# Attention mix on one core: free choice of engine for PSUM copies, planned PSUM banks, a reordered start and a split last tile

## Chip, cores, metric

The kernel runs on one core of a Trainium2 chip (trn2). The metric is device time in microseconds, the median of several executions. Short names: PE is the tensor engine (TensorE), PEld its weight loads, ACT is ScalarE, DVE is VectorE, POOL is GpSimd, SP is the queue that issues most DMAs. A "group" is the eight 128x512 matmuls that fill one PSUM bank.

All runs quoted here are in the fast state. Still, executions of one kernel differ by up to 0.9% here, and a part of the argument is about that. I use two measures side by side: the timed runs, and stretches between fixed landmarks of PE's instruction stream in the profiled run.

## The reference

```python
x = A_x; g = sigmoid((x * gate_w).sum(-1, keepdims=True))      # x: 1 x 2048 x 1024, bf16
a = linear_attention(x, A_wqkv, A_wo)    # 32 heads of 32; phi(t) = where(t > 0, t + 1, exp(t)) + 1e-6
#   kv = phi(k)^T v,  z = sum phi(k),  o = phi(q) kv / (phi(q) z + 1e-6),  a = o @ wo
b = local_attention(x, B_wqkv, B_wo)     # window of 8 keys at distance 2, softmax
return g * a + (1 - g) * b
```

## The kernel before

A small scheduler sorts operations: each has an engine, an assumed cost and what it reads and writes; the scheduler plays the program with these costs and emits each engine's order with semaphores. Program order gives priority. The parts that matter, with cuts:

```python
load_x(0, 0)                                   # x tiles come transposed, by SP
for d in range(0, 8, 2): load_w(0, 0, Bw, 2048, 1, d, d + 2, "act")   # first half of the v weights, 4 x 256 KB
for d in range(0, 8, 4): load_w(0, 1, Bw, 2560, 2, d, d + 4, "act")   # second half, 2 x 512 KB
for t in range(1, NT): load_x(t, 3 + t)
main = Ring(banks[0:7])                        # banks in rotation
for t in range(NT):                            # v of the local attention, both halves of a tile in turn
    for half in range(2): ...                  # a group, then copy to ACT (half 0) or DVE (half 1)
# ... gate matmuls ...
SO = banks[4:8]; OB = banks[3]                 # scores; fixed bank for P @ V
main = Ring(banks[0:3])                        # three rotating banks for the rest
def fill(e_, b, gr):                           # one block of the local attention
    # S: 16 row-tiled matmuls -> ACT exp -> DVE mask
    def values():
        db, _ = main.next()                    # P @ V into OB and the sums into db: one PE operation
        # ACT Ln, ACT Exp, DVE multiply into qT
    later.append((slot_n[0] + 2, values))      # two slots later
# k copies on ACT, q copies on DVE; after each tile of the linear attention: after(2, state)
# ... linear stage ...
for n, (u, j) in enumerate(nums):              # 32 numerator groups
    numer(u, j)      # group, phi (ACT exp, two DVE ops), DVE running maximum, later a "den" matmul, ACT Ln and Exp, DVE multiply
    if n == 3: turn()                          # transposes of kv, one DVE copy of 1024 columns
    if 6 <= n < 14: fold(n - 6, 0); fold(n - 6, 1)
    if n >= 17: a_out(*outs.pop(0))            # first output groups
# after(8 if u == 0 else 2, over): distance from a numerator to its den
# ... last stage: 16 tiles, each two groups, a DVE operation, a store
```

## Time and profile before

| | before |
|---|---|
| time, median of 3 runs at first | 519.6 us (519.31 to 521.1) |
| span of the profiled run | 518.7 us |
| PE busy | 504.4 us, 97% |
| first gate matmul (end of the v stage) | 67.01 us |
| kv transposes | 346.06 us |
| first output group | 375.79 us |

The page of the kernel before, first the engines' busy time, then the chain that ended last:

```profile
PE 504.4 (97%) x4385; PEld 229.8 (44%) x4385; DVE 276.3 (53%) x477; ACT 232.0 (45%) x342; POOL 4.7 (1%) x21
...
PE 92%; DVE 5%; DMA 2%; ACT 1%; ACTq 0%; issue 0%
```

PE is the bound. 256 groups at 1.73 us are 442 us of its time, and other matmuls are most of the remaining 62 us. No part of the change takes a matmul away, so everything must come from the 14.3 us of the span in which PE is idle (the start, waits, the tail) and from time lost inside its busy share (half clock, changes of mode, waits that the profile does not list). All of PE's waits, in total, number of times, and the longest:

```profile
PE ps_all L1253 <- DMA w_4_52<-in_B_wqkv_dram: 3.0, 2, 2.1
PE ps_all L1253 <- ACT ra_54_102 L1523: 1.8, 3, 1.1
PE ps_all L1284 <- DVE warm_72 L1203: 1.3, 1, 1.3
PE ps_all L1253 <- DMA xT_49<-in_A_x_dram: 0.9, 1, 0.9
PE ps_all L1253 <- DVE pk_46_94 L1262: 0.7, 1, 0.7
PE ps_all L1253 <- DVE pk_47_95 L1262: 0.7, 1, 0.7
PE ps_all L1521 <- DVE p_51_99 L1262: 0.5, 1, 0.5
PE ps_all L1253 <- ACT L_37_85 L1381: 0.3, 1, 0.3
PE ps_all L1253 <- DVE kva_68 L1451: 0.2, 1, 0.2
```

w_4 and xT are the start; pk, L and kva belong to the attention stage (a group waits until a bank has been read out); ra and p belong to the linear stage. The start itself, PE's timeline in the first 14 us (start, duration, what, and the idle time ahead of it):

```profile
6.02 1.04 PE L1253 MATMUL ps_all<-w_4_52,xT_49 128*128 128x512 bf16 x4 [0.88 <-DMA xT_49<-in_A_x_dram]
7.99 0.78 PE L1253 MATMUL ps_all<-w_4_52,xT_49 128*128 128x512 bf16 x2 [0.93 <-DMA w_4_52<-in_B_wqkv_dram]
10.87 3.59 PE L1253 MATMUL ps_all<-w_4_52,xT_49 128*128 128x512 bf16 x8 [2.10 <-DMA w_4_52<-in_B_wqkv_dram]
```

Eight matmuls from 10.87 us on take 3.59 us, twice their usual time: the clock had dropped. The window table shows it in the column before the DMA share (granted clock, 1.00 is full):

```profile
6.00:11.70 5.70, 2.65 (x9) 0.66 (x10) 0.00 (x0) 0.00 (x0) 0.00 (x0) 0.70 1.17 201
11.70:14.80 3.10, 3.10 (x9) 1.09 (x8) 0.00 (x0) 0.60 (x1) 0.00 (x0) 0.50 1.21 305
```

Not all waits are listed as such, since the ends of matmuls are modelled. In the timeline a tiled block of 16 is followed 0.22 us later by a block of its own mode (tiled in the same way) and 0.31 to 0.32 us later by one of another mode. Here the last one is followed only 0.55 us later (257.99 to 258.54 us), which I read as a hidden wait of 0.23 us; the profile names no cause for it.

```profile
257.57 0.38 PE L1443 MATMUL ps_all<-az_48_96,pk_46_94 128*32 128x33 bf16 x32
257.78 0.40 PE L1372 MATMUL ps_all<-E_33_81,v_38_86 128*32 128x114 bf16 x16
257.99 0.40 PE L1376 MATMUL ps_all<-E_33_81,ones_58 128*32 128x114 bf16 x16
258.54 0.82 PE L1253 MATMUL ps_all<-w_4_52,xT_49 128*128 128x512 bf16 x3
```

In the linear stage the other engines are full. The window from the kv transposes to the first output group (columns: window, its length, PE, PEld, DVE, ACT, POOL busy, clock, DMA): DVE is busy 29.43 of 29.73 us.

```profile
346.06:375.79 29.73, 27.34 (x128) 11.56 (x127) 29.43 (x66) 27.34 (x50) 0.00 (x0) 1.00 0.00 1
```

### The profile page before, as it was taken

Reading aid. Unit: us, or ns where it says so; the run is one execution under the profiler, and the core shown is the slowest. Engines: PE = TensorE matmul, PEld = TensorE weight load, DVE = VectorE, ACT = ScalarE, POOL = GpSimd, SP = SyncE. Lnnn points to the kernel's source line nnn. Section 1 sums busy time; section 2 is a strip of 40 time slices with the busy share of each in tenths; the row PEclk is TensorE's granted clock in tenths of the full one; section 3 lists DMA queues with packets and bytes.
Section 4 is the critical chain, followed back from the end, with each engine's and each line's share of the span. In section 5 each row is a group of like instructions: output and inputs, shape, how many; then the busy total and the mean of one; then the engine's idle time right before and its main releaser. Section 6 shows DMA issues by size and latency. Waiting matters only on the chain.

```text
span 518.7 us, 9927 instructions
## 1 busy us (share of the span) xinstructions
PE 504.4 (97%) x4385; PEld 229.8 (44%) x4385; DVE 276.3 (53%) x477; ACT 232.0 (45%) x342; POOL 4.7 (1%) x21
## 2 busy tenths in 40 slices
PE   6999999999999999999999999998999999999996
PEld 1444444444444444444444444443344444444442
DVE  0122235567676778466454544369986664334443
ACT  1111111355555567677675755348975653210000
POOL 3000000000000000000000000000000000000000
PEclk8999999999999999999999999999999999999999
DMA  9998790003300023001010100310000000002212
GB/s 201 209 236 297 232 323 3 2 22 101 104 21 21 23 92 123 23 13 32 13 32 11 33 11 3 126 38 1 0 2 0 2 0 1 1 23 81 82 65 81
DMA packets 47227, 34.81 MB, mean 67 GB/s; under 512 B 21957, under 2 KB 43205, under 8 KB 47178
## 3 DMA queue, kind: packets, MB, share of 16 engines
q1 hardware_dynamic: 45034, 32.01, 21.5%
q10 hardware_dynamic: 2144, 2.10, 1.6%
q8 instruction: 36, 0.59, 0.5%
q14 instruction: 13, 0.11, 0.1%
HBM read 21.51 MB, written 8.40 MB: 58 GB/s over the span
## 4 chain that ended last, share of the span: by engine, by line
PE 92%; DVE 5%; DMA 2%; ACT 1%; ACTq 0%; issue 0%
PE ps_all L1253 84%; PE ps_all L1354 2%; PE ps_all L1372 2%; DMA w_4_52<-in_B_wqkv_dram 2%; PE ps_all L1376 1%; PE ps_all L1443 1%; PE ps_all L1521 1%; DVE mx_57_105 L1211 1%; DVE w_5_53 L1281 1%; DVE pq_8_56 L1525 1%; DVE pq_8_56 L1262 1%; PE ps_all L1313 0%; ACT e_27_75 L1259 0%; DVE xT_49 L1525 0%; DVE kva_68 L1451 0%; DVE e_27_75 L1260 0%
## 5 line engine op out<-in xcount | busy, mean ns | idle before, releaser
L1253 PE MATMUL ps_all<-w_4_52,xT_49 128*128 128x512 bf16 x512 | 118.2, 385 | 5.9 <-DMA w_4_52<-in_B_wqkv_dram 3.0
L1253 PE MATMUL ps_all<-xT_49,w_6_54 128*128 128x512 bf16 x512 | 119.2, 380 | 1.8 <-ACT ra_54_102 L1523 1.8
L1253 PEld LDWEIGHTS ps_all<-w_4_52,xT_49 128*128 128x128 bf16 x512 | 48.9, 98 | 67.4 <-DMA w_4_52<-in_B_wqkv_dram 4.2
L1253 PEld LDWEIGHTS ps_all<-xT_49,w_6_54 128*128 128x128 bf16 x512 | 48.2, 98 | 60.6 <-ACT ra_54_102 L1523 3.5
L1253 PE MATMUL ps_all<-w_7_55,xT_49 128*128 128x512 bf16 x256 | 60.5, 380 | 0.3 <-ACT L_37_85 L1381 0.3
L1253 PE MATMUL ps_all<-xT_49,w_5_53 128*128 128x512 bf16 x256 | 58.6, 379 | 0.0
L1253 PE MATMUL ps_all<-w_7_55,qT_50 128*128 128x512 bf16 x256 | 55.4, 379 | 0.0
L1279 ACT ACTIVATE kT_51<-ps_all 128x512 bf16<-128x512 f32 x32 | 19.1, 597 | 60.5 <-PE ps_all L1253 60.5
L1253 PE MATMUL ps_all<-w_5_53,xT_49 128*128 128x512 bf16 x192 | 42.7, 379 | 0.0
L1253 PEld LDWEIGHTS ps_all<-w_7_55,qT_50 128*128 128x128 bf16 x256 | 25.0, 98 | 30.2
L1253 PEld LDWEIGHTS ps_all<-xT_49,w_5_53 128*128 128x128 bf16 x256 | 24.4, 98 | 29.4 <-issue 0.4
L1253 PEld LDWEIGHTS ps_all<-w_7_55,xT_49 128*128 128x128 bf16 x256 | 23.5, 98 | 27.7 <-ACT L_37_85 L1381 0.5
L1417 DVE TENSOR_SCALAR qT_50<-ps_all 128x512 bf16<-128x512 f32 x32 | 22.0, 688 | 13.6 <-PE ps_all L1253 13.4
L1253 PEld LDWEIGHTS ps_all<-w_5_53,xT_49 128*128 128x128 bf16 x192 | 18.8, 98 | 22.7
L1359 ACT ACTIVATE E_33_81<-ps_all 128x1824 bf16<-128x1824 f32 x12 | 20.2, 1687 | 4.7 <-PE ps_all L1354 4.6
L1211 DVE TENSOR_TENSOR mx_44_92<-mx_44_92,kT_51 128x1024 bf16<-128x1024 bf16 x16 | 11.0, 690 | 21.1 <-ACT kT_51 L1279 21.1
L1359 ACT ACTIVATE E_34_82<-ps_all 128x1824 bf16<-128x1824 f32 x12 | 20.2, 1686 | 2.1 <-PE ps_all L1354 2.1
L1359 ACT ACTIVATE E_35_83<-ps_all 128x1824 bf16<-128x1824 f32 (+1 forms) x12 | 20.1, 1677 | 2.1 <-PE ps_all L1354 2.1
L1259 ACT ACTIVATE e_25_73<-ps_all 128x512 bf16<-128x512 f32 x22 | 13.1, 596 | 17.4 <-PE ps_all L1253 17.4
L1451 DVE TENSOR_TENSOR kva_68<-ps_all,kva_68 128x264 f32<-128x264 f32 x15 | 6.5, 433 | 26.3 <-PE ps_all L1443 26.3
L1362 DVE TENSOR_TENSOR E_35_83<-E_35_83,msk_59 128x1824 bf16<-128x1824 bf16 (+1 forms) x12 | 13.2, 1100 | 12.4 <-ACT E_35_83 L1359 12.4
L1259 ACT ACTIVATE e_26_74<-ps_all 128x512 bf16<-128x512 f32 x21 | 12.5, 597 | 15.9 <-PE ps_all L1253 15.9
(156 smaller groups left out, 521.6 us busy)
## 6 DMA issues: line engine op xcount, KB each, us to landing
w_5_53<-in_B_wqkv_dram SPq DMA_DIRECT2D x2, 1024.0 KB, 7.5
w_6_54<-in_B_wqkv_dram SPq DMA_DIRECT2D x2, 1024.0 KB, 7.7
w_7_55<-in_A_wqkv_dram SPq DMA_DIRECT2D x2, 1024.0 KB, 6.0
w_4_52<-in_A_wqkv_dram SPq DMA_DIRECT2D x2, 1024.0 KB, 10.1
w_5_53<-in_A_wo_dram SPq DMA_DIRECT2D x2, 1024.0 KB, 5.7
w_6_54<-in_A_wqkv_dram SPq DMA_DIRECT2D x2, 1024.0 KB, 5.9
w_7_55<-in_B_wo_dram SPq DMA_DIRECT2D x2, 1024.0 KB, 6.5
out_dram<-o_55_103 SPq DMA_DIRECT2D x8, 256.0 KB, 2.0
```

The lines of the kernel that those rows point to most:

```text
L1211: P.op("dve", lambda e, m=m, op=op: e.tensor_tensor(m[:, 0:n], m[:, 0:n], src, op), 0.08 + n / 1920.0, reads=[m.all(), reg], writes=[m.all()],
L1253: last = e.matmul(bank.ap(), lhs(dc), rhs(dc), start=(dc == 0), stop=(dc == 7))
L1259: P.op("act", lambda e: e.activation(e_[:, :], bank.ap(), ACT.Exp), act(512), reads=[bank.iv], writes=[e_.all()])
L1262: P.op("dve", lambda e: e.scalar_tensor_tensor(out=dst, in0=bank.ap(), scalar=0.0, in1=e_[:, :], op0=ALU.max, op1=ALU.add), dps(512), read ...
L1279: P.op("act", lambda e: e.activation(dst, bank.ap(), ACT.Copy), act(512), reads=[bank.iv], writes=[reg])
L1281: P.op("dve", lambda e: e.tensor_copy(dst, bank.ap()), dps(512), reads=[bank.iv], writes=[reg])
L1354: last = e.matmul(SO[j].ap(c * nq, (c + 1) * nq), kT[32 * j:32 * j + 32, c0 + c, t0 + k0:t0 + k0 + 128], qT[32 * j:32 * j + 32, c0 + c, t0 ...
L1359: P.op("act", lambda e: e.activation(E[:, :, 0:nq].rearrange("p (j c) q -> p j c q", j=4), ps[:, 4:8, 0:4 * nq].rearrange("p j (c q) -> p ...
L1362: P.op("dve", lambda e: e.tensor_tensor(E[:, :, 0:nq], E[:, :, 0:nq], msk[:, mi:mi + 1, 0:nq].to_broadcast([128, 16, nq]), ALU.mult), 0.15 ...
L1372: e.matmul(OB.ap(c * nq, (c + 1) * nq)[32 * j:32 * j + 32, :], vt[:, (4 * c + j) * 32:(4 * c + j) * 32 + 32], E[:, 4 * j + c, 0:nq], start ...
L1417: P.op("dve", lambda e, dst=dst, bank=bank: e.tensor_scalar(dst, bank.ap(), SCALE, None, op0=ALU.mult), dps(512), reads=[bank.iv], writes= ...
L1451: P.op("dve", lambda e: e.tensor_tensor(kva[:, :, :], src(), kva[:, :, :], ALU.add), dps(264), reads=[bank.iv, kva.all()], writes=[kva.all()])
```

## The change

The intent: let no PSUM copy wait for a busy engine and no group for a bank. A copy goes to ACT or DVE, whichever the scheduler finds free first; banks come from a pool by an earlier pass of the plan (up to six passes); PV and sums are two operations; the scheduler charges for mode changes of PE; v starts with first halves only; the last tile is split. Cut to its core, indentation aside:

```diff
+        def ready(o, at):
+            if o.eng == "any":          # engine chosen when the operation becomes ready
+                ...
+                o.eng = min(est)[1]
...
+                if o.mode != mode:
+                    t += 0.09
...
-    for d in range(0, 8, 2):
-        load_w(0, 0, Bw, 2048, 1, d, d + 2, "act")
-    for d in range(0, 8, 4):
-        load_w(0, 1, Bw, 2560, 2, d, d + 4, "act")
+        load_w(0, 0, Bw, 2048, 0.1, 0, 2, "act")
+        load_w(0, 0, Bw, 2048, 0.2, 2, 4, "act")
+        load_w(0, 0, Bw, 2048, 0.3, 4, 6)
+        load_w(0, 0, Bw, 2048, 0.4, 6, 8)
...
+        for t, half in [(4 * b + i, half) for b in range(NT // 4) for half in range(2) for i in range(4)]:
...
+            if (t, half) == (0, 0):
+                load_w(0, 1, Bw, 2560, 1, 0, 4, "act", [o])      # only after the first group
+                load_w(0, 1, Bw, 2560, 2, 4, 8, "act", [o])
...
-    OB = banks[3]
-    main = Ring(banks[0:3])
+        main = Pool(banks[0:4])
...
-        later.append((slot_n[0] + 2, values))
+            after(3, values, True)
...
-                after(2, lambda t=t, pkt=pkt, azt=azt: state(t, pkt, azt))
+                    states.append((slot_n[0] + 4, lambda t=t, pkt=pkt, azt=azt: state(t, pkt, azt)))
...
+            for i in range(2):           # kv transposes leave PSUM in two copies
+                move(kvT[:, 4 * i:4 * i + 4, :].rearrange("p i c -> p (i c)"), ...
...
-        top((2,), p_, preg, 512)         # running maximum on DVE
+            phi(bank, p_, preg, 8 * u + j)   # accumulated by ACT's exponential instead
...
-        after(8 if u == 0 else 2, over)
+            after(6 if u == 0 else 2, over)
...
-        if n == 3:
+            if n == 1:
             turn()
-        if 6 <= n < 14:
+            if 3 <= n < 11:
...
+            parts = [(0, 512), (512, 1024)] if t < NT - 1 else [(0, 512), (512, 768), (768, 1024)]
```

The one-line description of the change did not mention the changed distances (three slots, four slots, `n == 1`, folds from 3) nor the maxima. The rate at which blocks of the local attention are handed out (`FILL`) went from 0.34 to one third per slot. A slot is one step of the program, one group of k, q or the linear stage.

## The prediction

> **What bounds it now.** TensorE. The page shows PE busy 504.4 of 518.7 us; the chain that ended last is 92% PE. By the table of forms and the timeline, the dense work is 256 groups of eight 128x512 matmuls at 1.73 us, 442 us. The change removes none of them. What can shrink:
>
> 1. Start. The waits give 3.9 us for the first weights and x tile. Continuous work begins at 10.87 us, and by the window table the granted clock is 0.50 from 11.7 to 14.8 us: nine matmuls at 427 ns, 1.9 us lost. The Trainium skill ("TensorE: Matmul & The Clock Gate", the HAM clock gate) has an idle window drop the clock to half[...].
> 2. Attention stage, 195 to 330 us: recorded PE waits of 1.9 us (ACT L, pk, kva) and three more inside "busy" (a 16-matmul block followed after 0.55 instead of 0.32 us). PE waits for one of three rotating banks, or PV's fixed bank.
> 3. Linear stage, 346 to 370 us: 8 groups and 30 single matmuls need 20.3 us (estimate from 1.73 and 0.216 us) and take 23.7. The chain here is a string of DVE operations.
> 4. Tail: the last matmul ends at 514.3 us; 0.75 us of DVE, a DMA and the closing follow.
>
> **What the change does.**
> - Start: the first four half tiles need 1 MB of weights, not 2, and the second half is issued only after the first group. Two pieces go behind x0 on the other queue. The first group should finish near 8 instead of 11.7 us. But four x tiles are now wanted 1.73 us apart while the second half competes; at the 202 GB/s of the first 13 us, 3 MB are not in before 14 us. I expect new short waits on xT and w. Net gain 3.0 us (1 to 5).
> - Attention: sums and PV become two operations on banks of one pool of four; values come a slot later, state two. I expect 2.0 us of the 2.6.
> - Linear: 32 running maxima leave DVE (0.43 us each here, 14 us), replaced by accumulation in ACT's exponentials; four R tiles, not two; folds go to either engine. ACT plus DVE then just fit beside PE. Gain 2.0 us.
> - Tail: last DVE step on 256 columns, 0.3 us.
> - Mode switches: the instruction order has 147 instead of 144 changes among plain, row-tiled and column-tiled matmuls, though the scheduler now charges for them. Each costs about 0.1 us (a 16-matmul block lasts 0.22 us before its own mode, 0.32 before another). The skill ("TensorEngine Tiling", Key Properties) says changing mode drains the engine; the trace agrees. Cost 0.3 us.
> - Choosing ACT or DVE for k, q and v copies gains nothing: PE does not wait between 16 and 195 us.
>
> **Sum.** 519.6 - 3.0 - 2.0 - 2.0 - 0.3 + 0.3 = 512.6 us, 1.3% faster; range 509.0 to 515.8. Faster by over 2%: 0.15; within 2%: 0.84; slower: 0.01.
>
> **What would show it.** Right: PE busy nearly unchanged; group one ends near 8 us, short PE waits on xT or w before 18 us, gate matmuls 3 us before 67.1; waits for pk, kva, L under 1 us in all; kv transposes to first output group 2 us shorter. Wrong: PE waits beyond 20 us; attention gaps stay; ACT leads the chain after 330 us (accumulating exponentials well over 0.75 us).
>
> **What would make it wrong.** The start is the largest and least certain term: if second-half weights starve the x tiles, it gains nothing; if the clock stays full and transfers overlap well, 5 us. The planned order rests on fixed costs; if they are off, new waits appear elsewhere.

## The result

The changed kernel took 512.84 us (512.26 to 514.8, 4 runs) against 519.77 us (519.31 to 521.1, 4 runs). The ratio is 0.9869, 95% interval 0.9836 to 0.9903. Ratios here are the mean time of one kernel's runs over that of the other's of the same rounds, so not quite the ratio of the medians. The prediction of 512.6 us holds.

The page of the changed kernel, the same parts:

```profile
PE 502.4 (98%) x4393; PEld 231.4 (45%) x4393; DVE 277.6 (54%) x462; ACT 224.3 (44%) x359; POOL 4.7 (1%) x21
...
PE 95%; DMA 2%; SPq 1%; DVE 1%; ACT 0%; issue 0%
```

All of PE's waits:

```profile
PE ps_all L1315 <- DMA xT_49<-in_A_x_dram: 4.3, 3, 3.4
PE ps_all L1354 <- DVE warm_72 L1265: 1.3, 1, 1.3
PE ps_all L1570 <- ACT kvT_94 L1347: 0.7, 1, 0.7
```

The waits of the attention stage are gone, and one is left in the linear stage. In the start, waits for weights have been traded for waits for x tiles:

```profile
5.93 2.00 PE L1315 MATMUL ps_all<-w_4_52,xT_49 128*128 128x512 bf16 x8 [0.66 <-DMA xT_49<-in_A_x_dram]
8.17 5.35 PE L1315 MATMUL ps_all<-w_4_52,xT_49 128*128 128x512 bf16 x24 [0.24 <-DMA xT_49<-in_A_x_dram]
16.91 5.44 PE L1315 MATMUL ps_all<-w_4_52,xT_49 128*128 128x512 bf16 x18 [3.38 <-DMA xT_49<-in_A_x_dram]
```

The first group ends at 7.9 us, as predicted, and four groups run at full clock. Then PE waits 3.38 us for the fifth x tile, which took 8.43 us to land (in the chain: start, duration, what), and the clock drops to half again after 16 us (same columns as above):

```profile
8.35 8.43 DMA xT_49<-in_A_x_dram
```

```profile
15.00:16.00 1.00, 0.00 (x0) 0.00 (x0) 0.00 (x0) 0.00 (x0) 0.00 (x0) 1.00 1.75 216
16.00:16.90 0.90, 0.00 (x0) 0.02 (x1) 0.00 (x0) 0.00 (x0) 0.00 (x0) 0.70 0.80 162
16.90:18.00 1.10, 1.09 (x3) 0.41 (x4) 0.00 (x0) 0.00 (x0) 0.00 (x0) 0.50 1.17 260
```

The linear stage, from kv transposes to first output group:

```profile
339.74:370.38 30.64, 29.98 (x146) 13.56 (x145) 26.91 (x53) 27.59 (x62) 0.00 (x0) 1.00 0.00 1
```

The two kernels run different numbers of numerator groups before these landmarks (7 and 5 before the transposes, 11 and 13 between transposes and first output group). So I subtract 1.727 us for each and call what is left A (gate matmuls to transposes) and L (transposes to first output group):

| stretch of the profiled run, us | before | changed | difference |
|---|---|---|---|
| start to first gate matmul | 67.01 | 66.75 | -0.26 |
| A | 266.96 | 264.36 | -2.60 |
| L | 10.73 | 8.19 | -2.54 |
| first output group to the end | 142.91 | 142.42 | -0.49 |
| span | 518.7 | 512.8 | -5.9 |

The profiled run of the changed kernel is the slowest of its four (514.8 us); the others have spans of 510.3 to 511.3 us at a clock of 0.999 or 1.000, the profiled one 0.995.

L has a floor: 0.44 us of transposes, then 16 folds and 15 denominators at 0.216 us, 7.13 us (with the 16 denominators of the changed kernel 7.35). So the kernel before lost 3.6 us there, the changed one 0.8, most of it the 0.66 us for kvT.

### The profile page after: what moved, and what is told of

Its sections match the earlier page's. It is cut to its first block, busy times and chain, and to the rows that moved or that the text cites. A ratio compares the mean times of both kernels' runs of the same rounds, so it can differ in the third digit from the quotient of the medians.

```text
span 512.8 us, 9938 instructions
## 1 busy us (share of the span) xinstructions
PE 502.4 (98%) x4393; PEld 231.4 (45%) x4393; DVE 277.6 (54%) x462; ACT 224.3 (44%) x359; POOL 4.7 (1%) x21
## 4 chain that ended last, share of the span: by engine, by line
PE 95%; DMA 2%; SPq 1%; DVE 1%; ACT 0%; issue 0%
PE ps_all L1315 75%; PE ps_all L1667 11%; PE ps_all L1444 4%; PE ps_all L1426 2%; DMA xT_49<-in_A_x_dram 2%; PE ps_all L1592 1%; SPq L1287 1%; PE ps_all L1513 1%; PE ps_all L1570 1%; DVE pq_8_56 L1328 0%; PE ps_all L1386 0%; DVE zbd_67 L1552 0%; SPq L1292 0%; DVE kvbd_66 L1553 0%; ACT e_25_73 L1324 0%
## 5 line engine op out<-in xcount | busy, mean ns | idle before, releaser
L1315 PE MATMUL ps_all<-w_4_52,xT_49 128*128 128x512 bf16 x512 | 117.1, 383 | 4.3 <-DMA xT_49<-in_A_x_dram 4.3
L1315 PE MATMUL ps_all<-xT_49,w_6_54 128*128 128x512 bf16 x512 | 118.3, 379 | 0.0
L1315 PEld LDWEIGHTS ps_all<-w_4_52,xT_49 128*128 128x128 bf16 x512 | 48.7, 98 | 64.3 <-issue 5.9
L1315 PE MATMUL ps_all<-w_7_55,xT_49 128*128 128x512 bf16 x256 | 59.7, 380 | 0.1
L1315 PE MATMUL ps_all<-xT_49,w_5_53 128*128 128x512 bf16 x256 | 58.6, 379 | 0.0
L1667 PE MATMUL ps_all<-w_7_55,qT_50 128*128 128x512 bf16 (+1 forms) x264 | 55.4, 373 | 0.0
L1315 PE MATMUL ps_all<-w_5_53,xT_49 128*128 128x512 bf16 x192 | 42.7, 379 | 0.0
L1347 ACT ACTIVATE kT_51<-ps_all 128x512 bf16<-128x512 f32 x19 | 11.3, 597 | 32.1 <-PE ps_all L1315 32.1
L1350 ACT ACTIVATE qT_50<-ps_all 128x512 bf16<-128x512 f32 x19 | 11.3, 597 | 29.9 <-PE ps_all L1315 29.9
L1349 DVE TENSOR_SCALAR xT_49<-ps_all,g_63 128x512 bf16<-128x512 f32 x15 | 11.2, 750 | 19.9 <-PE ps_all L1315 19.9
L1346 DVE CAST kT_51<-ps_all 128x512 bf16<-128x512 f32 x13 | 9.0, 689 | 17.4 <-PE ps_all L1315 17.4
L1434 DVE TENSOR_TENSOR E_38_86<-E_38_86,msk_59 128x1824 bf16<-128x1824 bf16 x12 | 13.2, 1103 | 5.7 <-ACT E_38_86 L1431 5.7
L1350 ACT ACTIVATE xT_49<-ps_all,g_63 128x512 bf16<-128x512 f32 x9 | 6.2, 687 | 22.9 <-PE ps_all L1315 22.9
```

The costliest lines, as they stand in the source:

```text
L1315: last = e.matmul(bank.ap(), lhs(dc), rhs(dc), start=(dc == 0), stop=(dc == 7))
L1346: fd = lambda e: e.tensor_copy(dst, src())
L1347: fa = lambda e: e.activation(dst, src(), ACT.Copy)
L1349: fd = lambda e: e.tensor_scalar(dst, src(), scale, None, op0=ALU.mult)
L1350: fa = lambda e: e.activation(dst, src(), ACT.Copy, scale=scale)
L1434: P.op("dve", lambda e: e.tensor_tensor(E[:, :, 0:nq], E[:, :, 0:nq], msk[:, mi:mi + 1, 0:nq].to_broadcast([128, 16, nq]), ALU.mult), 0.15 ...
```

## The experiments

Twelve kernels ran, all with correct results. Their edits are shown cut to the lines that matter. They ran in four sets, on three chips, each beside the kernel before, so compare ratios rather than medians. "Gate to end" is the span less the time of the first gate matmul; it leaves the start out. The kernel before has 451.7 us, the changed kernel 446.05.

| run | time, median (range), us | ratio to before | gate | A | L | gate to end |
|---|---|---|---|---|---|---|
| changed | 512.84 (512.26 to 514.80) | 0.9869 | 66.75 | 264.36 | 8.19 | 446.05 |
| e1_old_start | 514.76 (514.68 to 515.25) | 0.9903 | 67.07 | 264.36 | 8.19 | 446.1 |
| e2_paced | 512.09 (511.43 to 514.27) | 0.9869 | 63.06 | 265.18 | 7.34 | 446.3 |
| e3_keep_warm | 512.81 (511.95 to 513.18) | 0.9869 | 64.14 | 264.37 | 8.18 | 445.9 |
| e4_fixed | 514.14 (512.80 to 515.36) | 0.9893 | 64.85 | 263.73 | 8.43 | 445.9 |
| e5_pv_bank | 513.85 (2 runs) | 0.9874 | 66.64 | 264.11 | 7.19 | 445.4 |
| e6_old_slots | 518.53 (2 runs) | 0.9963 | 66.93 | 266.76 | 8.58 | 449.2 |
| e7_mx_back | 516.84 (2 runs) | 0.9931 | 66.87 | 264.35 | 9.31 | 447.2 |
| e9_linear_old | 513.88 (2 runs) | 0.9874 | 65.98 | 264.72 | 7.14 | 445.8 |
| b1_positions | 517.30 (516.92 to 517.33) | 0.9944 | 66.22 | 265.26 | 10.00 | 449.1 |
| b2_halves | 518.01 (517.03 to 519.99) | 0.9959 | 68.62 | 265.27 | 10.15 | 449.3 |
| e10_pace8 | 512.65 (512.18 to 513.03) | 0.9858 | 64.05 | 264.37 | 8.19 | 446.4 |
| e11_best | 510.84 (510.06 to 514.69) | 0.9837 | 63.26 | 264.11 | 7.13 | 445.0 |

One caution holds for all of them: every edit makes the scheduler plan the whole order anew. e2 touches only the start, yet its A is 0.82 us longer and its L 0.85 us shorter than in the changed kernel. So a difference in A or L of that size need not come from the line that was edited.

### e1_old_start: the changed kernel with the old start

```diff
-        load_w(0, 0, Bw, 2048, 0.3, 4, 6)       # and the other three of this kind
+        for d in range(0, 8, 2): load_w(0, 0, Bw, 2048, 1, d, d + 2, "act")
+        for d in range(0, 8, 4): load_w(0, 1, Bw, 2560, 2, d, d + 4, "act")
-            if (t, half) == (0, 0):             # and its two loads
-        for t, half in [(4 * b + i, half) for b in range(NT // 4) for half in range(2) for i in range(4)]:
+        for t, half in [(t, half) for t in range(NT) for half in range(2)]:
```

> The changed kernel with the old start: loads, prompt second half of the weights, and both halves of one tile after another. Theory: the start is worth 0.3 us where the clock dropped after the 3.4 us wait for the fifth x tile (as in the profiled run of the changed kernel: gate matmuls at 66.75 against 67.08 us) and about 2.4 us where it did not. So here the gate matmuls start at 66.9 to 67.3 us, granted clock about 0.992, time 514.0 to 514.6 us (changed kernel 512.3 to 512.9), and the times of its runs scatter less than the changed kernel's. Rival: the new start is worth its 3 us always, and the profiled run only misread it: then 515.5 or more.

Measured: gate at 67.07 us, A and L exactly as in the changed kernel, 514.76 us, and all four runs within 0.6 us. So the new start is worth about 1.8 us in the timed runs (0.9903 less 0.9869, times 519.7 us), between the two figures expected; the intervals of the two ratios overlap (0.9888 to 0.9919 here), so this is rough. That the new start brings the scatter is not shown: the kernel before has the old start, and its nine runs of the same rounds spread over 1.9 us (519.28 to 521.16). The rival (3 us always) falls. The granted clocks were 0.993 to 0.999, so my figure of 0.992 was no constant.

### e2_paced: second half of the weights in quarters

```diff
-            if (t, half) == (0, 0):
-                load_w(0, 1, Bw, 2560, 1, 0, 4, "act", [o])
-                load_w(0, 1, Bw, 2560, 2, 4, 8, "act", [o])
+            if half == 0 and t < 4:
+                load_w(0, 1, Bw, 2560, 1 + t, 2 * t, 2 * t + 2, "act", [o])
```

> The changed kernel, but the second half of the v weights is loaded in four quarters of 256 KB, one after each of the first four groups, not as 1 MB after the first. Theory: the wait of 3.38 us for the fifth x tile comes from the 1 MB crowding out the transposed x loads (issue to landing 8.4 us against a median of 4.3); paced, no PE wait for x or w after 8 us exceeds 1.7 us, the clock stays at 1.0, the gate matmuls start at 63.5 to 65 us and the time is 509.5 to 511.0 us. Rival: the x tiles are late because their issues take 1.3 us each on their queue, or all bytes are needed anyway: then the waits only move, the gate starts no earlier than 66 us and the time stays at 512 to 513.

Measured: in the profiled run the start is 3.7 us earlier (gate at 63.06 us), and the longest wait for x is 1.04 us:

```profile
7.90 9.57 PE L1315 MATMUL ps_all<-w,xT 128*128 128x512 bf16 x42 [0.20 <-DMA xT<-in_A_x_dram]
18.51 5.77 PE L1315 MATMUL ps_all<-w,xT 128*128 128x512 bf16 x26 [1.04 <-DMA xT<-in_A_x_dram]
```

The fifth x tile was issued at 8.1 us and landed at 13.12 us, not at 16.78. So the 1 MB of weights beside the x loads did cause the long wait there. But the profiled run (511.43 us) is the fastest of five; the median is 512.09 and the ratio the changed kernel's. Mechanism seen, gain in time not shown. This run also refutes a simple account of the scatter: its slowest run, 514.27 us, had a granted clock of 1.000, and so had the slowest run of the kernel before (521.16 us).

### e3_keep_warm: eight idle-time matmuls in the long wait

```diff
+            if (t, half) == (3, 0):
+                P.op("pe", lambda e: [e.matmul(banks[7].ap(), warm[:, 0:128], warm[:, :], ...) for i in range(8)][-1], 8 * mm(512),
+                     reads=[warm.all()], writes=[banks[7].iv], after=[o])
```

> The changed kernel with eight idle-time matmuls of 128x512 on the warm-up tile after the fourth group, where PE waits 3.38 us for an x tile; they cost 1.73 us of a wait that is there anyway. Theory: the wait lets the granted clock fall to half for about 4 us in some runs, and that is worth 1.9 us; with the fill the clock is 1.0 in every run, the gate matmuls start at 64.4 to 65.2 us, the times lie within 511.8 to 512.6 us and scatter less than the changed kernel's 512.3 to 514.8. Rival: the scatter has nothing to do with the clock: same spread, gate at 66.5 or later.

Measured: gate at 64.14 us; the fill runs from 13.06 us, and the wait after it is 0.75 us:

```profile
13.06 1.89 PE L1374 MATMUL ps_all<-warm 128*128 128x512 bf16 x8
15.70 8.58 PE L1315 MATMUL ps_all<-w,xT 128*128 128x512 bf16 x39 [0.75 <-DMA xT<-in_A_x_dram]
```

No run had a clock under 0.998, and none was slower than 513.18 us. The median, however, is 512.81, the changed kernel's: three of its four runs had a clock of 0.999 or 1.000, so there was a drop to take away in one run only. Four runs against one outlier are few. In e4 to e9, which have the same start, 11 of 13 runs had a clock of 0.997 or less, and the four of these that were traced (e5, e6, e7, e9) show the drop in a wait of 2.33 to 3.70 us; there the fill might be worth more, which was not tried. The expected range of all times (511.8 to 512.6) was missed on the upper side.

### e4_fixed: every PSUM copy on its old engine

```diff
-            P.op("any", {"act": fa, "dve": fd}, ...
+            P.op(eng, fa if eng == "act" else fd, ...         # v by half, k ACT, q DVE, kvT DVE, folds and outputs alternating
```

> The changed kernel with every PSUM copy on the engine it had before (v alternating by half, k on ScalarE, q on VectorE, the transposes on VectorE, folds alternating, outputs alternating), all else as changed. Theory: PE never waited for these copies before 195 us, and in the linear stage the gain came from the running maxima taken off VectorE, so the choice of engine is worth under 0.5 us: 512.3 to 513.4 us, and PE waits between 67 and 370 us of at most 1.5 us in all. Rival: the free choice of engine is what removed the waits in the attention and linear stages: then 514.5 to 517 us, with waits of 2 us or more there.

Measured: gate to end 445.9 us, the changed kernel 446.05; PE waits after the gate 0.8 us (ra 0.5, kva 0.3). So the free choice of engine, the headline of the change, shows no gain after the start. The median of 514.14 us is above the expectation. I put that down to the start, though only the run of 512.80 us was traced: two runs at a clock of 1.000 took 512.80 and 512.95 us, three at 0.995 to 0.997 took 514.14 to 515.36. The rival needed 2 us of waits in the later stages; they are not there. Whether the choice of engine for v makes the drop of the clock rarer, these few runs don't say.

### e5_pv_bank: a fixed bank for PV, three for the rest

```diff
-        main = Pool(banks[0:4])
+        main = Pool(banks[0:3])
+        obs = Pool(banks[3:4])
-                ob = main.next()
+                ob = obs.next()
```

> The changed kernel with the attention stage's four shared banks split again into three rotating ones and one fixed for PV; slots as changed. Measured from the first gate matmul to the transposes of kv, less 1.727 us for each numerator group run in between: 266.96 us before, 264.36 changed. Theory: the shared pool is what removed the PE waits; so here 265.5 to 267 us, with 1.5 us or more of PE waits between 195 and 335 us. Rival: the later slots (next run) did it, and here it stays within 264.1 to 264.9 us. From the gate to the end of the span: 451.65 before, 446.05 changed; here 447 to 448.5 by the theory.

Measured: A is 264.11 us, no PE wait at all in the attention stage, gate to end 445.4. My theory fell: sharing four banks shows no gain.

### e6_old_slots: values two slots later, states two slots later

```diff
-            after(3, values, True)
+            after(2, values, True)
-                    states.append((slot_n[0] + 4, ...
+                    states.append((slot_n[0] + 2, ...
```

> The changed kernel with the old distances: values two slots after the scores instead of three, the kv state two slots after its tile instead of four; banks as changed. Gate to transposes less numerator groups: 264.36 us changed. Theory (pool of banks): 264.2 to 265.2 us; the instruction order has 155 mode changes instead of 147, at 0.1 us each 0.8 us. Rival (later slots did it): 265.5 to 267 us with PE waits for pk, L or kva of 1.5 us or more.

Measured: A is 266.76 us, as in the kernel before. PE's waits after the start:

```profile
PE ps_all L1426 <- ACT E L1431: 1.4, 1, 1.4
PE ps_all L1570 <- ACT kvT L1347: 0.8, 1, 0.8
PE ps_all L1315 <- ACT ra L1594: 0.3, 1, 0.3
```

Of the 2.40 us, 1.4 is the wait for E, and eight more mode changes (155 against 147 in the instruction order) are about 0.8 us at 0.1 each. The rival is right: the later slots make the difference in the changed kernel, though by a wait of another kind than it named, and partly by mode changes.

### e7_mx_back: running maxima on DVE again

```diff
-            phi(bank, p_, preg, 8 * u + j)
+            phi(bank, p_, preg)
+            top((2,), p_, preg, 512)
```

> The changed kernel with the 32 running maxima back on VectorE and the accumulation taken out of ScalarE's exponentials; four R tiles and free copies as changed. From the kv transposes to the first output group, less 1.727 us for each numerator group in between: 10.73 us before, 8.19 changed. VectorE was 99% busy there before (29.43 of 29.73 us) and is 88% busy now. Theory: the maxima on VectorE were the limit; here 9.3 to 10.5 us and VectorE over 94% busy. Rival: the R tiles or the free choice of engine did it: here 8.1 to 8.8 us.

Measured: L is 9.31 us, 1.12 more, with a wait for p (a DVE result) of 0.7 us, and DVE is busy 30.33 of 31.76 us, 95%. This is at the edge of what my theory expected, and hardly more than e2 moved L without touching the maxima.

### e9_linear_old: maxima, two R tiles and fixed engines together

The R tiles (`ra` in the waits) are the buffers in which ACT makes the reciprocals of the denominators.

```diff
+            top((2,), p_, preg, 512)                           # as in the run before
-  enumerate((Er.t[0], Er.t[1], Lr.t[0], vr.t[0]))
+  enumerate((Er.t[0], Er.t[1]))
+            P.op(eng, fa if eng == "act" else fd, ...          # as in the run with fixed engines
```

> As the run before, and also two R tiles instead of four and every PSUM copy on its old engine: the linear stage as before in all but its slots. Transposes to first output group less numerator groups: theory 10.3 to 11.2 us (10.73 before), so that this run less the run before gives the share of R tiles and free copies, expected under 1 us. Rival: if the maxima alone are the cause, equal to the run before within 0.2 us.

Measured: L is 7.14 us, at its floor, and gate to end 445.8 us. Both the theory and the rival missed. With all three parts undone at once the linear stage is no slower; it is faster than with one. So none of them is what made the gain, and the maxima on DVE (99% busy in the window of before) were not by themselves the limit: here DVE is busy 28.63 of 29.59 us, 97%, and PE doesn't wait. In e7 they cost 1.1 us beside the free choice of engines, here nothing. The two runs differ in two more parts, so why is not settled. What shows in the traces is that PE runs a numerator group between transposes and folds here and doesn't wait for kvT at all. First the changed kernel, then e9:

```profile
339.74 0.61 PE L1560 MATMUL ps_all<-ident_57,kvbd_66 128*128 128x128 bf16 x8
340.18 0.38 PE L1592 MATMUL ps_all<-pq_8_56,zbd_67 128*128 128x512 bf16 x1
341.23 1.04 PE L1570 MATMUL ps_all<-w_5_53,kvT_94 128*128 128x512 bf16 x4 [0.66 <-ACT kvT_94 L1347]
```

```profile
339.34 0.61 PE L1561 MATMUL ps_all<-ident,kvbd 128*128 128x128 bf16 x8
339.79 1.89 PE L1316 MATMUL ps_all<-xT,w 128*128 128x512 bf16 x8
341.52 1.03 PE L1571 MATMUL ps_all<-w,kvT 128*128 128x512 bf16 x4
```

### b1_positions: the kernel before with the new distances alone

```diff
-        later.append((slot_n[0] + 2, values))
+        later.append((slot_n[0] + 3, values))
-                after(2, lambda t=t, pkt=pkt, azt=azt: state(t, pkt, azt))
+                after(4, lambda t=t, pkt=pkt, azt=azt: state(t, pkt, azt))
-        after(8 if u == 0 else 2, over)
+        after(6 if u == 0 else 2, over)
-        if n == 3:
+        if n == 1:
-        if 6 <= n < 14:                # and fold(n - 6, ...)
+        if 3 <= n < 11:                # and fold(n - 3, ...)
```

> The kernel before with nothing but the changed distances: values three slots after the scores and the kv state four after its tile (two and two before), kv transposes after the second numerator (fourth before), folds from the fourth (seventh before), denominators of the first chunk six slots behind (eight before). Banks, engines, maxima, R tiles and start as before. The runs so far say that the fixed PV bank costs nothing and that old slots cost 2.4 us, and that maxima, R tiles and fixed engines together do not bring the old linear stage back. New theory: the distances alone made both gains. Attention stage (gate to transposes less numerators) 263.8 to 264.8 us (266.96 before, 264.36 changed), linear stage (transposes to first output group less numerators) 7.2 to 9 us (10.73 before, 8.19 changed), gate to end 446 to 447.5 us (451.65 before), time 514 to 516 us. Rival: the planned order over a pool of banks is needed as well: then at least one of the stages stays within 1 us of the kernel before, and the time at 516.5 or more.

Measured: gate to end 449.1 us, 2.6 of the 5.6 us that separate the two kernels. A is 265.26 (1.7 of 2.6 us), L is 10.00 (0.7 of 2.5). PE's waits after the start:

```profile
PE ps_all L1497 <- DVE kvT L1492: 1.8, 1, 1.8
PE ps_all L1253 <- ACT L L1381: 1.4, 4, 0.3
PE ps_all L1522 <- DVE p L1262: 0.7, 1, 0.7
PE ps_all L1253 <- ACT az L1466: 0.4, 1, 0.4
```

The new theory (distances alone) fell; the rival's figures hold, so something of the changed kernel besides the distances is needed. Part of what the distances do is mode changes: in the trace PE changes mode 135 times here and 144 times in the kernel before, about 0.9 us at 0.1 each. The four waits for L are for banks in rotation: the next bank in turn is still held by the chain of ACT operations. The changed kernel, and e5 with only three banks, show none of them.

### b2_halves: besides, the kv transposes copied in halves

```diff
-        P.op("dve", lambda e: e.tensor_copy(kvT[:, :, :]..., bank.ap().bitcast(BF16)), dps(1024), ...
+        for i in range(2):
+            P.op("dve", ... kvT[:, 4 * i:4 * i + 4, :] ... [:, 512 * i:512 * i + 512]), dps(512), ...
```

> The run of changed distances on the kernel before, and besides the transposes of kv leave PSUM in two copies of 512 columns instead of one of 1024 (both on VectorE as before). In that run the first fold waited 1.77 us for the one copy; in the changed kernel, with two copies, it waits 0.66 us, and in the run with the old linear parts not at all. Theory: the copy in halves is most of what the distances left open in the linear stage: transposes to first output group less numerators 8.0 to 9.2 us (10.0 with distances alone, 8.19 changed), longest PE wait on kvT under 1.2 us. Rival: the wait only moves to the next bank, since VectorE stays full with the 32 maxima and the pool and plan are missing: 9.6 us or more.

Measured: L is 10.15 us, the wait for kvT 1.5 us instead of 1.8, and others took the rest. The theory fell. In b1 DVE starts the copy 1.03 us after the transposes' end (341.76 against 340.73 us) and takes 0.68 us for it, so DVE's operations ahead of the copy are the larger part of PE's wait.

### e10_pace8 and e11_best: a start over eight tiles

```diff
-        for t, half in [(4 * b + i, half) for b in range(NT // 4) for half in range(2) for i in range(4)]:
+        for t, half in [(8 * b + i, half) for b in range(NT // 8) for half in range(2) for i in range(8)]:
-            if (t, half) == (0, 0):            # and its two loads
+            if half == 0 and t < 8 and t % 2 == 0:
+                load_w(0, 1, Bw, 2560, 1 + t, t, t + 2, "act", [o])
```

> The changed kernel with its start over eight tiles: the first halves of v of eight tiles, then the second halves, and the second half of the weights in quarters after groups 1, 3, 5 and 7. Theory: at the start PE lives on the x tiles as they land (1.73 us a group, 256 KB a tile), and the second half must only trickle in; no wait for x after 8 us exceeds 1 us, gate matmuls at 62.5 to 64 us, time 509.5 to 511.5 us, scatter under 1.5 us. Rival: the transfers carry about 215 GB/s in the first 20 us whatever the order, and with PE at their heel each hiccup shows: gate 64 to 66.5 us, times scattering over 2 us, median 511.5 to 513.

> The run before with PV on its own fixed bank again, since that run had the shortest stretch from gate to end (445.36 against 446.05 us). Theory: gains add: 0.3 to 0.8 us below the run before. Rival: 445.36 was chance or only moved work past the first output group: equal within 0.3 us.

Measured for e10: no wait for x after 8 us above 0.5 us, clock 0.999 to 1.000 in all runs, scatter 0.85 us as the theory had it; but the gate is at 64.05 us and the median 512.65, as the rival had it. PE now waits for the second half of the weights (1.04 us at 22.8 us), as most bytes are needed anyway.

Measured for e11, the same start with e5's banks: 1.3 us less from gate to end (445.0 against 446.4), nearly all in L, which comes to its floor: the order has a numerator group between transposes and folds again, and there is no wait for kvT. That is more than expected. I lay it to the plan's order and not to the PV bank as such: e2, without that bank, has the same order there and an L of 7.34 us. 510.84 us is the lowest median of all, ratio 0.9837 (0.9808 to 0.9865), but one of six runs took 514.69 us, and the interval overlaps the changed kernel's.

## Why the prediction was right

The total was right by terms that were off in both directions, so coming within 0.3 us of the median is in part luck. Point by point:

- **PE bound, nothing to gain from its work.** Right: 504.4 and 502.4 us busy.
- **Start, "net gain 3.0 us (1 to 5)".** Mis-sized. The profiled run gained 0.26 us, the timed runs about 1.8 (e1). The first group did end at 7.9 us. The failed step is the size of the new waits: one of 3.38 us for the fifth x tile, caused by the second half of the weights beside it (e2), and in some runs a half clock after it. In the two runs with a span of 510.3 us (clock 0.999 and 1.000) the gate would be at about 64.3 us, 2.7 us earlier, if the rest takes its 446.05 us (an estimate from those two spans): without the drop the term nearly holds. The x tile took 8.43 us from issue to landing, against a median of 4.3 us. "Gate matmuls 3 us before 67.1" was wrong for the profiled run of the changed kernel; e2 and e11 reach it.
- **Attention, "2.0 us of the 2.6".** It was 2.60, all of it, and no wait for pk, kva or L is left. I had laid it to the pool of four banks and the later slots. The pool's sharing shows no gain (e5); the slots are worth 1.7 us on the kernel before (b1) and 2.4 in the changed one (e6), by waits and by 8 or 9 mode changes fewer. The choice of bank by plan instead of rotation explains the rest only by elimination: b1 waits 1.4 us for banks in rotation, e5 picks three by plan and doesn't; the changed `FILL` and the scheduler's charge for modes are not ruled out.
- **Linear, "Gain 2.0 us".** It was 2.54. The step "ACT plus DVE then just fit beside PE" is not supported: with the maxima back on DVE, the other linear parts undone and DVE 97% busy, L is at its floor (e9). The distances alone give 0.7 us (b1), copying in halves nothing (b2). What gives the other 1.8 us is left open: of what I did not isolate, the pool of eight banks, the repeated planning and the changed waits in the scheduler remain, and the order that the plan happens on moves L by 0.85 us by itself (e2).
- **Free choice of engine "gains nothing".** Right (e4), and also for the folds and outputs, of which I had not said so.
- **Tail, 0.3 us.** Right: from the start of the last DVE operation to the end 4.36 us before (518.7 less 514.34), 4.07 changed (512.8 less 508.73).
- **Mode changes, cost 0.3 us.** Never isolated; e6 with eight more fits 0.1 us each. The Trainium skill ("TensorEngine Tiling", Key Properties) says a change of mode drains the engine; the 0.22 and 0.32 us of the trace agree.

## What to carry to other kernels

When one engine is 97% busy, sum its few gaps by stage and by what ends them, and compare stages between landmarks with equal work; terms in both directions can add up to the right total. A change with a headline (free engines, shared banks) can owe its gain to small lines beside it, here how many slots later a consumer comes: undo parts one by one, and several together, before believing either. An engine that starts sooner on data that still trickles in meets its waits later (here 3.38 us for the fifth x tile), so the gain can be smaller than the earlier start. And where a planner orders the program, an edit moves more than the lines it touches (e2).

## What the Trainium skill lacked or had wrong

- "ScalarE: Activation LUTs" says that an ACTIVATE can give an accumulator output, and nothing of its cost. Here it is an instruction of its own on ACT, 0.20 us after each exponential, 6.4 us for 32:

```profile
L1324 ACT ACTIVATE e_26_74<-ps_all 128x512 bf16<-128x512 f32 x8 | 4.8, 601 | 3.9 <-PE ps_all L1315 3.9
...
L1324 ACT ACTIVATION_READ_ACCUMULATOR e_26_74<-ps_all 128x1 f32 x8 | 1.6, 204 | 0.0
```

- "TensorEngine Tiling" (Key Properties) names the drain at a change of mode, without a size: about 0.10 us here.
- "DMA: Bandwidth & Descriptors" (Queues, rings and completion order) says that the engines go round the queues packet by packet. What follows for transposed loads it doesn't say: in the first 30 us of the kernel before, the SP queue (q1: the transposed x tiles and three stores of v) moved 279 bytes a packet, the weights on ACT's queue (q10) 979, by the table below (queue, packets, MB, share). A bulk load on the other queue fits the slow fifth x tile; that this is by packet size is inferred, not tested, and so is that the profile's packets are those of the page.

```profile
q1 hardware_dynamic: 14512, 4.05, 81.1%
q10 hardware_dynamic: 2144, 2.10, 28.3%
```

- "TensorE: Matmul & The Clock Gate" (The HAM clock gate) has, in its table of the two states, about 3.4 us of idleness drop the clock. A wait of 3.38 us in the changed kernel did (0.70 in the last 0.9 us of it), one of 2.65 us in e4 did not, and one of 2.33 us in e9 did (0.72 between 15.5 and 16.0 us, 0.50 after). So the length of the wait alone doesn't decide. And the kernel before dropped between 8.0 and 8.5 us (0.79 there, 0.50 after) with no gap over 0.93 us since its warm-up matmuls began: PE had been busy 1.05 us between 6 and 8 us. So light work didn't keep the clock up here, and for the drop in the kernel before the trace does not agree with that row.
